# A rewritten instruction order for the first 19 steps of a fused attention and feed-forward kernel

## Chip, core and metric

The kernel runs on one NeuronCore of a Trainium2 chip, as one launch. The metric is the device time of that core in microseconds (us), taken as the median of several runs. Beside the timed runs there is one execution under the hardware profiler, which gives the trace.

## What is computed

Linear attention on eight batches of eight heads, followed by a feed-forward layer over all 4608 rows, in fp32:

```python
q_s = softmax(q, axis=-1)            # exp(q - max) / (sum + 1e-9), over the head dimension
k_s = softmax(k, axis=2)             # over the sequence, 576 rows
kv  = einsum('bhsd,bhse->bhde', k_s, v)
x   = einsum('bhsd,bhde->bhse', q_s, kv)      # -> rows (4608, 512)
h   = x @ w_in                       # (4608, 2048)
g   = h - tanh(h)
out = g @ w_out                      # (4608, 512)
```

The shapes are q, k, v (8, 8, 576, 64), w_in (512, 2048) and w_out (2048, 512). Both weights arrive as 64-bit floats and are split on the chip into a high and a low part.

## The kernel before

**Tiling.** The rows are cut into nine chunks j of 512. For each chunk there are 16 steps f, each of 128 columns of w_in and the matching 128 rows of w_out. Every product of the feed-forward layer is made of three matmuls (high by high, high by low, low by high), so one step is 12 matmuls `ph` (h_mm, x times a piece of w_in) and, two steps later, four groups of three matmuls `po` (o_mm, g times a piece of w_out), one group for each tile of 128 rows. The steps run in this order: chunk 0 with f from 0 to 7, chunk 1 with f from 0 to 15, chunk 0 with f from 8 to 15 (its first half is set aside in DRAM, `ev` and `sv`, and fetched back), then chunks 2 to 8. In the names below ph9 is the ph group of step 9, which is chunk 1 with f=1.

**Names of the parts.** One word of the order is one part of the work, and each part runs on one engine:

- PE (TensorE): `warm13` (13 dummy matmuls), `pm`, `pb`, `pk` (maximum, its broadcast, and k times v of one batch), `pt` (transposes of q), `px` (q times kv), `ph`, `po`.
- SP (SyncE) issues all DMAs: `k0.1`, `q3`, `v1.0` and `ld.i4` (a piece of w_in; `ld.o4` of w_out), `sv`.
- DVE (VectorE): `km`, `mx`, `mh`, `ml` (maximum of k), `ks` (k minus it), `mq`, `sq`, `sa`, `sr` (softmax of q), `sl`, `rs`, `rc`, `kn` (normalising kv), `xl`, the split of a weight (`cl`, `st`), and of each step `g`, `tt`, `gg`, `cp`.
- ACT (ScalarE): `qe`, `ke` (exponentials), `qs`, `xh`, `ev` (copies out of PSUM), the split of a weight (`pr`, `lo`, `ca`), and of each step `u`, `t`, `vv`, `m`, `gh`.
- DVE or POOL (GpSimd): `qu`, `qn`, `sub` (low part of a weight), `gl` (low part of g). A star behind the word puts it on DVE, no star on POOL.

**What sets the order.** ORDER, a list of 576 words, is issued word by word under `tc.manual_schedule` for all five engines; each engine gets its words in this order and executes them in this order, waiting in front of each for its inputs and its buffer. It covers steps 0 to 16 (`PLANNED = 17`) and the split of all 32 weight pieces. From step 17 on only PE and SP keep the written order; the instructions of DVE, ACT and POOL are placed by a planner, which is free to put them between those of ORDER. The attention of chunk 2 (batch 2, and the tile `q_rest`) is written at steps 19.5 to 32 by prepare(2, ...), and the planner places its DVE, ACT and POOL work wherever its inputs are early.

**Buffers that matter.** PSUM has eight banks: two for `ph` (ps_h), four for `po` (ps_o, which before the first `po` hold `pt` and `px`), two for the attention (ps_m). A ph group can begin when the one before the last has been read by u, t, m, g and tt. The step's tiles u, t, g, gh, gl have two buffers each, vv and mk one, the split weights' c three. v_load contains the memset of the ones beside the values (on POOL) and then issues the DMA of the values (on SP).

Of the kernel before, what the change touches and what calls it, by code (L numbers as in the profile page):

```python
# [44 lines left out]
tt4 lo.o7 lo.o6 ld.o8 cp3 qe3 km1.c gh3 cl.o4 ld.o12 km1.d m4 t5 sq3 gl3 ph6 pr.o4 ld.o11 u5 tt5
lo.i9 cl.i7 lo.i8 gg4 ld.o13 pr.i7 st.o4 po3 vv5 cp4 ca.o4 st.i7 ld.i12 gh4 qu2* u6 m5 pm1 gl4*
qe2 ld.i11 mx1 ca.i7 sub.o4* t6 sq2 sub.i7 po4 ld.o9 lo.o11 lo.i12 g5 lo.o8 mh1 cl.o5 lo.o13
ld.o10 ml1 gg5 pr.o5 sa2 pb1 sa3 cp5 vv6 sr2 ld.i10 lo.i11 sr3 ph7 qn5 ks1.0 gh5 m6 gl5 ks1.1
ke1.0 ld.i13 ks1.2 lo.o9 qn6 pk1.0 ke1.1 tt6 qn7 g6 pt6 ke1.2 pk1.1 qs6 st.o5 ld.o15 t7 qn4*
ca.o5 pt5 cl.o6 pk1.2 u7 sub.o5* qs5 ld.i15 sl1 gg6 po5 pr.o6 rs1 lo.i13 cp6 vv7 rc1 st.o6 gh6  # L50
kn1 ca.o6 cl.o7 pt4 m7 g7 sub.o6 pt7 qs4 tt7 qs7 gl6* pr.o7 px6 lo.o15 gg7 lo.i15 st.o7 po6
ld.i14 xh6.0 cp7 xh6.1 xl6.0 gh7 xl6.1 ca.o7 gl7* lo.o10 px4 sub.o7* lo.i10 lo.o12 cl.i8 cl.i9
po7.0 xh4.1 ld.o14 cl.o8 xh4.0 cl.o9 po7.1 xl4.1 pr.i8 xl4.0 pr.i9 po7.2 st.i8 pr.o8 ph8 st.i9
ev.1 ca.i8 cl.o11 sv.1 cl.i11 ca.i9 sub.i8 pr.i11 lo.o14 po7.3 sub.i9* t8 ph9 cl.i13 u8 tt8 m8
g8 vv8 cl.i10 ev.3 gg8 pr.i10 sv.3 cl.o14 ev.2 cp8 ph10 t9 sv.2 st.i10 gh8 tt9 m9 gl8* u9 pr.o14
st.o8 po8.0 t10 g9 vv9 po8.1 tt10 u10 gg9 ph11 ca.o8 g10 vv10 cp9 pr.o9 gg10 gh9 sub.o8* m10
po8.2 gl9* t11 ph12 u11 cp10 ev.0 g11 m11 sv.0 tt11 vv11 cl.o12 ca.i10 gg11 pr.o11 po8.3
sub.i10* u12 ph13 cp11 gh10 st.o11 vv12 gl10* m12 st.i11 t12 pr.o12 g12 po9 t13 tt12 u13 gg12
ca.i11 tt13 vv13 sub.i11 lo.i14 ph14 gh11 cp12 ca.o11 gl11 m13 pr.i13 sub.o11 g13 po10 u14 t14
gg13 tt14 vv14 cp13 ph15 st.o12 gh12 cl.i14 m14 gl12* ca.o12 cl.o15 pr.i14 g14 pr.o15 st.i14  # L60
po11 u15 gg14 t15 sub.o12* ca.i14 cp14 vv15 tt15 m15 ph16 sub.i14* gh13 cl.i12 gl13* pr.i12
st.o14 g15 ca.o14 po12 st.i12 t16 u16 gg15 ca.i12 sub.o14 tt16 vv16 cp15 gh14 sub.i12 m16 gl14*
# [7 lines left out]
def attn_moe_kernel(  # L70
# [533 lines left out]
    def h_step(j: int, f: int):  # L604
        parts = h_parts(j, f)
        last = None
        eng = nc.vector if (j, f) == (NCH - 1, NF - 1) else nc.gpsimd
        for name, part in parts.items():
            if name == "last":
                last = part()  # L610
            elif name == "gl":
                part(eng)
            else:
                part()
        return last
# [120 lines left out]
    done = set()  # L736
    with tc.manual_schedule(engines={ENG.PE, ENG.DVE, ENG.Activation, ENG.Pool, ENG.SP}):
        for name in ORDER.split():
# [12 lines left out]
            done.add(name)  # L751

    pieces = [p for p in pieces if "sub.{}{}".format(*p) not in done]
    loaded = 0

    def pieces_upto(need: int, last):

        nonlocal loaded
        while len(pieces) > need:
            for kind, f in pieces[:2]:  # L760
                if f"ld.{kind}{f}" not in done:
                    ops[f"ld.{kind}{f}"]()
                    done.add(f"ld.{kind}{f}")
            kind, f = pieces.pop(0)
            for part in ("cl", "pr", "lo", "st", "ca", "sub"):
                with tc.issue_after(last.ins):
                    ops[f"{part}.{kind}{f}"](*((nc.gpsimd,) if part == "sub" else ()))
# [60 lines left out]
```

## Time and profile before

| | |
|---|---|
| median of 3 runs | 918.03 us (915.72 to 918.67) |
| profiled execution, device time | 920.28 us |
| its span, first to last instruction | 918.5 us |
| mean granted TensorE clock | 0.99 |
| PE busy | 890.2 us, 97% of the span |
| DVE busy | 615.4 us, 67% |
| ACT busy | 556.1 us, 61% |
| POOL busy | 288.2 us, 31% |

The shares are means over the whole run. The engines' load differs from stretch to stretch, so a view by stretches has to be read beside them. The 1.8 us between the span and the device time lie outside the program's instructions.

### The profile page before, as it was taken

Reading aid. Unit: us, or ns where it says so; the run is one execution under the profiler, and the core shown is the slowest. Engines: PE = TensorE matmul, PEld = TensorE weight load, DVE = VectorE, ACT = ScalarE, POOL = GpSimd, SP = SyncE. Lnnn points to the kernel's source line nnn. Section 1 sums busy time; section 2 is a strip of 40 time slices with the busy share of each in tenths; the row PEclk is TensorE's granted clock in tenths of the full one; section 3 lists DMA queues with packets and bytes.
Section 4 is the critical chain, followed back from the end, with each engine's and each line's share of the span. In section 5 each row is a group of like instructions: output and inputs, shape, how many; then the busy total and the mean of one; then the engine's idle time right before and its main releaser. Section 6 shows DMA issues by size and latency. Waiting matters only on the chain.

```text
span 918.5 us, 13209 instructions
## 1 busy us (share of the span) xinstructions
PE 890.2 (97%) x5034; PEld 721.9 (79%) x5034; DVE 615.4 (67%) x906; ACT 556.1 (61%) x967; POOL 288.2 (31%) x246
## 2 busy tenths in 40 slices
...
GB/s 254 317 305 118 95 82 1 9 61 92 1 126 47 103 1 58 115 12 24 46 61 67 24 46 24 115 0 16 79 24 1 1 70 12 0 1 46 1 1 46
DMA packets 79776, 57.47 MB, mean 63 GB/s; under 512 B 14689, under 2 KB 72033, under 8 KB 79713
## 3 DMA queue, kind: packets, MB, share of 16 engines
...
q14 instruction: 25, 0.20, 0.1%
...
## 4 chain that ended last, share of the span: by engine, by line
PE 77%; DVE 7%; ACT 5%; DMA 4%; issue 4%; POOL 2%; SPq 0%; DVEq 0%; ACTq 0%; POOLq 0%
PE po L635 37%; PE ph L544 35%; PE pk L299 2%; DMA k<-in_k_dram 2%; PE px L465 1%; PE pt L437 1%; DVE g L573 1%; DVE g L565 1%; DVE g L578 1%; DMA spare_q<-in_q_dram 1%; ACT gh L581 1%; DVE t L570 1%; DMA raw_o<-in_moe_w_out_dram 1%; POOL d L267 1%; DMA q<-in_q_dram 1%
## 5 line engine op out<-in xcount | busy, mean ns | idle before, releaser
L635 PE MATMUL po<-w_o,gh 128*128 128x512 f32 x1152 | 361.5, 395 | 1.5 <-DVE w_o L167 1.5
L544 PE MATMUL ph<-xh,w_i 128*128 128x512 f32 x1152 | 317.7, 398 | 10.3 <-ACT mk L559 6.0
L584 POOL TENSOR_TENSOR gl<-g,gh 128x512 fp32r<-128x512 f32 x130 | 172.6, 1328 | 389.7 <-ACT gh L581 373.5
L544 PEld LDWEIGHTS ph<-xh,w_i 128*128 128x128 f32 x1152 | 214.6, 190 | 59.3 <-ACT mk L559 7.3
L635 PEld LDWEIGHTS po<-w_o,gh 128*128 128x128 f32 x1152 | 214.7, 188 | 51.0 <-DVE w_o L167 1.8
L565 DVE SCALAR_TENSOR_TENSOR g<-u,ph 128x512 f32<-128x512 f32 x144 | 98.3, 682 | 219.2 <-ACT t L559 202.2
L635 PE MATMUL po<-w_o,gl 128*128 128x512 f32 x576 | 226.4, 393 | 1.5 <-DVE gl L584 1.5
L581 ACT CAST gh<-g 128x512 fp32r<-128x512 f32 x144 | 89.2, 620 | 177.7 <-DVE g L578 172.6
L544 PE MATMUL ph<-xl,w_i 128*128 128x512 f32 x576 | 157.9, 397 | 0.0
L559 ACT ACTIVATE u<-ph 128x512 f32<-128x512 f32 x144 | 85.8, 596 | 81.4 <-PE ph L544 81.1
L573 DVE SCALAR_TENSOR_TENSOR g<-vv,g 128x512 f32<-128x512 f32 x144 | 120.4, 836 | 20.0 <-ACT vv L559 10.4
L544 PEld LDWEIGHTS ph<-xl,w_i 128*128 128x128 f32 x576 | 109.8, 191 | 25.0 <-DVE xl L486 0.6
L635 PEld LDWEIGHTS po<-w_o,gl 128*128 128x128 f32 x576 | 108.1, 188 | 27.0 <-DVE gl L584 2.4
L578 DVE COPY_PREDICATED g<-mk,t 128x512 f32<-128x512 int32 x144 | 118.8, 825 | 3.3
L559 ACT ACTIVATE vv<-u,b_pa 128x512 f32<-128x512 f32 x144 | 104.5, 726 | 6.9 <-DVE g L573 6.8
L559 ACT ACTIVATE mk<-ph 128x512 int32<-128x512 f32 x144 | 86.2, 599 | 35.9 <-DVE g L565 32.3
L570 DVE TENSOR_TENSOR t<-ph,t 128x512 f32<-128x512 f32 x144 | 98.0, 681 | 4.0 <-ACT mk L559 3.1
L559 ACT ACTIVATE t<-ph 128x512 f32<-128x512 f32 x144 | 85.2, 592 | 1.1 <-PE ph L544 1.1
L389 POOL TENSOR_TENSOR q<-q,mq 128x1024 f32<-128x1024 f32 x14 | 27.7, 1979 | 47.5 <-DVE mq L384 44.6
L423 POOL TENSOR_TENSOR qn<-q,sq 128x512 f32<-128x512 f32 x28 | 31.9, 1142 | 28.1 <-DVE sq L403 14.6
L384 DVE TENSOR_REDUCE mq<-q 128x16 f32<-128x1024 f32 x15 | 18.2, 1216 | 23.9 <-DMA q<-in_q_dram 23.9
L167 POOL TENSOR_TENSOR w_i<-c_i,w_i 128x512 fp32r<-128x512 f32 x10 | 14.5, 1451 | 52.2 <-ACT w_i L163 42.6
...
## 6 DMA issues: line engine op xcount, KB each, us to landing
...
```

What stands on the lines that cost most here:

```text
L299: nc.tensor.matmul(st["pk"][hh * D : (hh + 1) * D, a, j : j + D + 1], kt[:, h, j] if u < NKP else kt[:, h], vt[:, h, j * (D + 1) : (j + 1) ...
L389: eng.tensor_tensor(qf, qf, mq, op=ALU.subtract)
L423: eng.tensor_tensor(qn.rearrange("p a g d -> p g a d"), qt[:, :, j].rearrange("p (g a) d -> p g a d", g=2), sq[:, :, j : j + 1] .broadcast ...
L544: nc.tensor.matmul(ph, w[:, i, c], x[:, c, :], start=(n == 0), stop=(n == len(ops) - 1))
L559: st["last"] = nc.scalar.activation(new(tag, **of), st[src], fn, **kw)
L565: nc.vector.scalar_tensor_tensor(new("g"), st["u"], C2, st["ph"], op0=ALU.mult, op1=ALU.mult)
L570: nc.vector.tensor_tensor(st["t"], st["ph"], st["t"], op=ALU.subtract)
L573: nc.vector.scalar_tensor_tensor(st["g"], st["vv"], PB, st["g"], op0=ALU.add, op1=ALU.mult)
L578: nc.vector.copy_predicated(st["g"], st["mk"], st["t"])
L581: nc.scalar.copy(new("gh", F32R), st["g"])
L584: eng.tensor_tensor(new("gl", F32R), st["g"], st["gh"].bitcast(F32), op=ALU.subtract)
L635: nc.tensor.matmul(po[t], g[:, cols], wt["o", f][:, w], start=(begin and n == 0), stop=(end and n == 2),)
```

## The change

ORDER is written anew. It now has 603 words and covers steps 0 to 18 (`PLANNED = 19`). The memsets of the ones become parts of their own (`vo`), which the order can place ahead of the loads `v`; the memset and the load stay the same instructions. From step 19 to step 31 every instruction of DVE, ACT and POOL is traced under `tc.issue_after` of the last ORDER instruction of its engine, so that the planner can't put it between those of ORDER; this holds for the attention of chunk 2. Two ph groups, of steps 2 and 3, take their PSUM bank from ps_o and not from ps_h. The dummy matmuls fall from 47 to 34 and take another pool once x exists. The function pieces_upto, which had nothing left to do since ORDER splits all 32 pieces, goes.

The core of the diff; of ORDER, the stretch from the start to the first po groups:

```diff
-k0.0 warm13 k0.1 q1 km0.a k0.2 km0.b q0 km0.c mq1 v0.1 km0.d qu1 pm0 v0.2 mq0 warm16 v0.0 mx0
-qu0 qe1 ld.i0 sq1 qe0 ld.o0 mh0 sa1 ml0 sr1 pb0 sq0 qn2 ld.i2 warm1 lo.i0 qn3 ks0.0 pt2 warm1
-qs2 sa0 pt3 ks0.1 ke0.0 ld.i1 warm2 qs3 ks0.2 pk0.0 ke0.1 sr0 ld.i3 cl.i0 qn0* pr.i0 pk0.1 cl.i2
-ke0.2 st.i0 pr.i2 ld.o2 pt0 cl.i1 ca.i0 qn1 pk0.2 lo.i2 warm1 sl0 sub.i0 pr.i1 ld.i4 rs0 pt1 rc0
-qs0 warm2 kn0 qs1 cl.i3 px2 lo.i1 cl.o0 ld.o1 st.i2 pr.o0 px0 st.i1 xh2.1 cl.o2 xh2.0 xl2.1
-ld.i5 ca.i1 warm11 xl2.0 xh0.1 xh0.0 sub.i1* ca.i2 xl0.1 ld.o3 lo.o0 sub.i2 xl0.0 pr.i3 ph0
-lo.i3 k1.0 cl.o1 lo.o1 st.o0 lo.i4 st.i3 ca.o0 cl.i4 ld.o4 cl.o3 ca.i3 sub.o0* pr.i4 ph1 sub.i3*
-u0 st.i4 k1.2 t0 ld.i6 vv0 g0 m0 tt0 ca.i4 gg0 ph2 v1.0 u1 sub.i4 t1 g1 vv1 tt1 lo.o2 ld.i7 gg1
-pr.o2 cp0 u2 st.o2 pr.o1 k1.1 cl.i6 gh0 st.o1 m1 gl0* t2 ph3 q3 cp1 ca.o2 ca.o1 cl.i5 sub.o2*
-gh1 sub.o1 g2 pr.i5 ld.o5 tt2 m2 po0 t3 gl1* vv2 v1.2 km1.a pr.i6 v1.1 gg2 pr.o3 km1.b u3 ph4
...
+vo0.1 q0 mq0 q1 k0.0 mq1 qu0 k0.1 km0.a qe0 sq0 qu1 k0.2 km0.b sa0 km0.c sr0 qe1 ld.i0 ld.i4
+vo0.0 km0.d warm13 pm0 qn0 lo.i4 sq1 lo.i0 mx0 sa1 ld.i2 mh0 sr1 q3 v0.0 ml0 cl.i0 cl.i4 pr.i0
+vo0.2 v0.1 v0.2 cl.i2 pr.i2 warm5 pb0 st.i0 pr.i4 ks0.0 ld.i1 ks0.2 lo.i2 qn1 ke0.0 ks0.1 mq3
+pt0 qn2 st.i2 qu3* warm4 pt1 ke0.2 ke0.1 st.i4 pk0.0 pk0.1 pk0.2 q2 k1.2 qs0 ca.i0 sl0 rs0 cl.i1
+qs1 pt2 ca.i2 qn3 vo1.0 rc0 qe3 lo.i1 kn0 ld.i3 vo1.2 pt3 ld.i5 sub.i2 sub.i0 sq3 qs3 k1.0 pr.i1
+qs2 k1.1 mq2 warm2 px0 px2 warm10 xh0.0 xh0.1 st.i1 qu2 xh2.1 ld.o0 xl0.0 xl0.1 xh2.0 xl2.1
+ca.i1 xl2.0 ld.o1 lo.i3 cl.i5 qe2 lo.i5 cl.i3 ca.i4 pr.i5 ph0 sa3 pr.i3 sub.i1 u0 ld.i6 sr3 m0
+sq2 sa2 km1.a sr2 st.i3 km1.b g0 ld.i7 ph1 km1.c vv0 ca.i3 t0 cl.o0 gg0 u1 pr.o0 km1.d ld.o2 t1
+lo.o0 tt0 cl.o1 vv1 lo.o1 cp0 st.o0 ph2 pm1 sub.i4 mx1 t2 g1 tt1 mh1 qn6 gg1 lo.i6 u2 ca.o0 ml1
+st.i5 gh0 m1 vo1.1 v1.0 cp1 vv2 qn4 pt6 ld.i10 sub.i3 qs6 ca.i5 ph3 qn5 t3 gl0 gh1 sub.i5 pb1
+ks1.2 ks1.0 m2 v1.1 ld.o3 tt2 gl1 ph4 ks1.1 lo.o2 pt4 g2 ke1.0 u3 ke1.2 cl.i7 gg2 qs4 cl.o2 tt3
+ke1.1 u4 vv3 cp2 cl.i6 g3 pr.o1 ld.o5 ph5 st.o1 m3 pr.o2 lo.o3 ca.o1 v1.2 gg3 pr.i6 cl.o3 st.o2
+pk1.0 ld.o4 lo.i7 cl.i10 sub.o1* ld.o10 t5 ld.i12 ca.o2 pt5 sub.o0 ld.o6 qs5 pk1.1 cp3 cl.o5 po0
...
     def warm(n: int):
-        t = ps_h.tile([P, P], F32, name="warm", tag="h")
+        pool, tag = ((ps_m, "m") if po else (ps_o, "o")) if xs else (ps_h, "h")
+        t = pool.tile([P, P], F32, name="warm", tag=tag)
...
-    def v_load(b: int, st: dict, u: int):
+    def v_ones(b: int, st: dict, u: int):
...
     def h_mm(j: int, f: int):
         xh, xl = xs[j]
-        ph = ps_h.tile([P, CH], F32, name=f"ph{j}_{f}", tag="h")
+        pool, tag = (ps_o, "o") if j == 0 and f in (2, 3) else (ps_h, "h")
+        ph = pool.tile([P, CH], F32, name=f"ph{j}_{f}", tag=tag)
...
-    PLANNED, SPREAD = 17, 3
+    PLANNED = 19
...
+            ins = nc.cur_bb.bb.instructions[-1]
+            if ins.engine in (ENG.DVE, ENG.Activation, ENG.Pool):
+                ends[ins.engine] = ins
...
-            last = h_step(j, f)
-            pieces_upto(max(0, left - (left * (n + 1 - PLANNED) + SPREAD - 1) // SPREAD), last)
+            with ExitStack() as behind:
+                for ins in ends.values() if n < 2 * NF else ():
+                    behind.enter_context(tc.issue_after(ins))
+                h_step(j, f)
```

The rest of the new order, by what the prediction uses: PE goes on with `pk1.2 po1 pt7 po2 ph6 px4 ph7 po3 px6 po4 ph8 po5 ph9 po6 po7.0 po7.1 ph10 po7.2 ph11 po7.3 po8.0 po8.1 po8.2 ph12 po8.3 ph13` and ends with `ph18 po15 po16`. POOL has 32 words other than memsets, against 30. DVE has 223, against 215, and ends with `gl18* sub.o15*`; ACT has 221, against 211, and ends with `gh18`.

## Rows read from the trace of the kernel before

**Rows 1.** The page: busy time, share of the span and instructions of each engine.
```profile
PE 890.2 (97%) x5034; PEld 721.9 (79%) x5034; DVE 615.4 (67%) x906; ACT 556.1 (61%) x967; POOL 288.2 (31%) x246
```

**Rows 2.** By stretch: length, busy of each engine (instructions), clock, DMA share, GB/s.
```profile
0.00:30.50 30.50, 23.24 (x266) 22.02 (x266) 20.38 (x36) 15.14 (x24) 10.82 (x19) 0.89 0.98 284
30.50:49.80 19.30, 15.08 (x50) 11.15 (x49) 17.60 (x28) 15.81 (x29) 4.20 (x6) 0.82 0.88 234
49.80:98.50 48.70, 45.27 (x326) 36.08 (x325) 45.92 (x79) 46.94 (x84) 14.85 (x13) 1.00 0.65 217
98.50:118.50 20.00, 17.09 (x64) 12.64 (x63) 16.88 (x28) 16.28 (x30) 0.80 (x1) 0.91 0.23 79
118.50:159.40 40.90, 39.39 (x170) 31.33 (x169) 37.51 (x58) 28.78 (x53) 12.61 (x9) 1.00 0.20 38
159.40:290.00 130.60, 126.25 (x720) 101.43 (x720) 91.23 (x126) 73.91 (x129) 49.26 (x40) 1.00 0.21 59
290.00:910.00 620.00, 620.00 (x3431) 504.45 (x3430) 383.80 (x552) 357.68 (x621) 195.67 (x160) 1.00 0.13 35
```

**Rows 3.** Chain that ended last, near 218 us: start, us, what.
```profile
217.69 2.72 PE ph L544 x12
```

**Rows 4.** Waits, 30 to 160 us: us in total, times, longest.
```profile
PE ph L544 <- ACT mk L559: 6.0, 3, 2.2
...
PE ph L544 <- DVE t L570: 2.0, 1, 2.0
...
DVE km L226 <- DMA k<-in_k_dram: 1.0, 1, 1.0
```

**Rows 5.** Timeline around the k load of batch 2: start, us, engine, line.
```profile
106.18 0.38 SPq L189 DMA_DIRECT2D k<-in_k_dram  x1
...
110.30 0.69 DVE L223 TENSOR_TENSOR km<-k 128x512 f32<-128x512 f32 x1 [1.08 <-DMA k<-in_k_dram]
...
112.26 0.62 ACT L581 CAST gh<-g 128x512 fp32r<-128x512 f32 x1 [1.33 <-DVE g L578]
...
113.43 1.36 PE L544 MATMUL ph<-xh,w_i 128*128 128x512 f32 x4 [2.09 <-ACT mk L559]
```

**Rows 6.** Two short stretches, columns as in Rows 2: ph12, then part of po15.
```profile
113.43:117.87 4.44, 4.44 (x12) 3.51 (x13) 3.78 (x7) 3.70 (x7) 0.00 (x0) 0.62 0.16 61
149.65:154.01 4.36, 3.05 (x13) 2.17 (x12) 4.26 (x7) 2.75 (x5) 1.29 (x2) 1.00 0.01 4
```

**Rows 7.** Timeline of the start, 0 to 31 us.
```profile
13.92 1.22 DVE L397 TENSOR_REDUCE sq<-spare_q 128x16 f32<-128x1024 f32 x1 [0.27 <-ACT spare_q L392]
...
23.86 0.68 PE L299 MATMUL pk<-vr,kr 64*64 64x65 f32 x16
...
27.95 2.72 PE L183 MATMUL warm<-ident 128*128 128x128 f32 x22
...
28.11 0.42 DVE L145 TENSOR_SCALAR raw_o<-raw_o 128x512 f32<-128x512 f32 x1
...
30.52 1.21 PE L544 MATMUL ph<-xh,w_i 128*128 128x512 f32 x4
```

**Rows 8.** Timeline of DVE and POOL at three places, 22 to 153 us.
```profile
22.90 1.21 DVE L156 SCALAR_TENSOR_TENSOR c_i<-raw_i 128x512 uint32<-128x512 uint32 x1 [0.19 <-ACT raw_i L149]
...
38.33 1.28 POOL L167 TENSOR_TENSOR w_i<-c_i,w_i 128x512 fp32r<-128x512 f32 x1 [5.90 <-ACT w_i L163]
38.38 1.77 DVE L573 SCALAR_TENSOR_TENSOR g<-vv,g 128x512 f32<-128x512 f32 x1
...
40.08 0.68 DVE L565 SCALAR_TENSOR_TENSOR g<-u,ph 128x512 f32<-128x512 f32 x1
...
41.28 0.68 DVE L573 SCALAR_TENSOR_TENSOR g<-vv,g 128x512 f32<-128x512 f32 x1
...
152.23 2.42 DVE L156 SCALAR_TENSOR_TENSOR c_o<-raw_o 128x512 uint32<-128x512 uint32 x2
```

**Rows 9.** Timeline of PE at the maximum of batch 2.
```profile
173.14 0.60 PE L235 MATMUL pm<-ident,km 128*128 128x128 f32 x4
```

More of the change, by code (lines that the diff above doesn't have):

```diff
@@ L45 @@
[L45 to L62, printed above, removed]
@@ new lines @@
+pr.o4 kn1 ld.o7 st.o3 px4 cl.o6 vv5 gh4 cl.i12 st.o4 ca.o3 gg5 ca.o4 xh4.1 sub.o3* st.o5 gl4* u6
+sub.i7 cp5 xl4.1 xh4.0 cl.o9 t6 ph7 u7 vv6 lo.o7 po3 xl4.0 tt6 t7 px6 ca.o5 gh5 g6 m6 xh6.0
+ld.i9 xh6.1 ld.i13 pr.o6 pr.i12 gg6 sub.o4 xl6.0 xl6.1 lo.i10 lo.o6 ld.o8 po4 cl.o12 cl.o7
+sub.o5* cp6 cl.i9 ld.i11 pr.o7 gl5 g7 ph8 st.o6 vv7 lo.i11 m7 ld.i15 tt7 gg7 po5 gh6 pr.i10 cp7
+gl6* st.i10 u8 ca.o6 st.o7 ph9 ld.i14 ld.i8 sub.o6* lo.i12 vv8 gh7 g8 po6 pr.i9 t8 lo.i15 t9 u9
+tt8 ca.o7 pr.o12 gg8 gl7* m8 sub.o7* vv9 lo.i9 po7.0 cl.i15 cl.i8 pr.i15 tt9 st.i12 cp8 ld.o15
@@ new lines @@
+cl.i13 lo.o10 ld.o11 po7.1 ld.o14 gh8 lo.i8 m9 st.i15 ph10 gl8* g9 cl.o15 ev.0 po7.2 cl.i14 sv.0
+gg9 ca.i12 u10 cl.o8 cp9 ph11 cl.i11 ev.2 ev.1 t10 ca.i15 vv10 g10 po7.3 tt10 po8.0 m10 sub.i15
+cl.o11 cl.o14 po8.1 pr.o10 gg10 t11 gh9 ev.3 u11 ca.i10 gl9* pr.o8 pr.i8 cp10 g11 po8.2 tt11
+vv11 m11 sub.i12 ph12 lo.o12 st.o10 gg11 st.i9 sub.i10 ca.o10 t12 lo.o8 lo.o14 st.i8 po8.3 gh10
+ph13 cp11 ca.i9 u12 m12 ld.o13 po9 ca.i8 lo.i14 t13 sub.i9* sub.o10* gl10* pr.i11 sv.3 tt12 vv12
+g12 st.o12 gh11 gg12 ca.o12 u13 st.i11 pr.o11 gl11* po10 cp12 pr.o9 m13 sub.o12 tt13 vv13 ca.i11
@@ new lines @@
+ph14 pr.i14 lo.i13 g13 gg13 po11 sub.i8* u14 sub.i11* cp13 gh12 gl12* t14 st.o8 ph15 lo.o9
+pr.o15 g14 sv.1 po12 m14 gh13 tt14 lo.o11 st.o9 vv14 ca.o8 ph16 gl13* gg14 pr.i13 u15 sv.2 vv15
+pr.o14 st.o11 g15 cp14 gh14 t15 sub.o8 lo.o15 u16 po13 m15 gg15 tt15 vv16 t16 cp15 ca.o11 gl14
+cl.o13 sub.o11 tt16 g16 ca.o9 st.i14 ph17 gg16 lo.o13 st.i13 gh15 po14 gl15* m16 ca.i14 cp16
+ca.i13 u17 g17 ph18 t17 sub.i13* st.o14 vv17 gg17 gh16 ca.o14 tt17 sub.o14* sub.o9* u18 po15
+gl16* t18 st.o15 tt18 po16 m17 pr.o13 ca.o15 vv18 st.o13 cp17 gh17 g18 sub.i14 gg18 m18 ca.o13
@@ L66 @@
+cp18 gl17* sub.o13* gh18 gl18* sub.o15*
 """
@@ L177, in attn_moe_kernel @@
     REST = S - 2 * P * NKP
+    gs = {}
+    po = {}
+    xs = {}
     def warm(n: int):
-        t = ps_h.tile([P, P], F32, name="warm", tag="h")
+        pool, tag = ((ps_m, "m") if po else (ps_o, "o")) if xs else (ps_h, "h")
+        t = pool.tile([P, P], F32, name="warm", tag=tag)
         for _ in range(n):
@@ L498, in prepare @@
                 put(0, lambda u=u: k_load(b, st, u))
-            put(0, lambda: v_load(b, st, 0))
-            put(0, lambda: v_load(b, st, NKP))
+            for u in (0, NKP):
+                for part in (v_ones, v_load):
+                    put(0, lambda u=u, part=part: part(b, st, u))
             for n in range(4):
@@ L509, in prepare @@
             put(KX + 7, lambda: kv_mm(b, st, 0))
-            put(KX + 7, lambda: v_load(b, st, 1))
+            for part in (v_ones, v_load):
+                put(KX + 7, lambda part=part: part(b, st, 1))
             put(KX + 10, lambda: kv_mm(b, st, 1))
@@ L558, in act @@
             of = {"dt": kw.pop("dt", F32)} | ({"bufs": kw.pop("bufs")} if "bufs" in kw else {})
-            st["last"] = nc.scalar.activation(new(tag, **of), st[src], fn, **kw)
+            nc.scalar.activation(new(tag, **of), st[src], fn, **kw)
         def ph():
@@ L605, in h_step @@
         parts = h_parts(j, f)
-        last = None
         eng = nc.vector if (j, f) == (NCH - 1, NF - 1) else nc.gpsimd
         for name, part in parts.items():
[L609 to L615, printed above, removed]
+            part(*((eng,) if name == "gl" else ()))
     dram = ctx.enter_context(tc.tile_pool(name="dram", bufs=1, space=bass.MemoryType.DRAM))
@@ L735, in attn_moe_kernel @@
     ENG = mybir.EngineType
-    done = set()
+    ends = {}
     with tc.manual_schedule(engines={ENG.PE, ENG.DVE, ENG.Activation, ENG.Pool, ENG.SP}):
@@ L750, in attn_moe_kernel @@
             ops[name](*eng)
[L751 to L767, printed above, removed]
+            ins = nc.cur_bb.bb.instructions[-1]
+            if ins.engine in (ENG.DVE, ENG.Activation, ENG.Pool):
+                ends[ins.engine] = ins
     calls = {}
```

38 lines of the change are left out of this document (17 added, 21 removed).

## The prediction

> **What bounds the kernel now.** I read the page first, then the busy time by stretch, the chain that ended last, the waits, and the timeline of the first 160 us. On the page PE is busy for 97% of the span, so only PE's idle and slow time can be won, and the question is where it lies [rows 1]. The stretches answer it: from 290 to 910 us PE has no idle time at all, in 620.0 us [rows 2]. Nothing there can be gained, and the change doesn't touch it. The losses lie ahead. At full clock a group of twelve matmuls takes 2.72 us [rows 3]. By that measure:
>
> - 30.5 to 49.8 us holds four ph groups, 10.9 us of work in 19.3, so 8.4 are lost. PE waits there for m and tt of the steps before, because only two PSUM banks serve ph, and the clock falls to a mean of 0.82 [rows 2, 4].
> - 49.8 to 98.5 us: 48.7 less 45.3 busy at clock 1.00, so 3.4 lost [rows 2].
> - 98.5 to 118.5 us: 64 matmuls, 14.5 us of work in 20.0, so 5.5 lost [rows 2].
> - 118.5 to 159.4 us: 40.9 less 39.4, so 1.5 lost [rows 2].
>
> That is 18.8 us between the first ph and the 17th po, beside 30.5 us ahead of the first ph. From 159.4 to 290 us another 4.3 are idle [rows 2]. In the stretch from 49.8 to 98.5 us ACT is busy for 46.9 of 48.7 us and DVE for 45.9 [rows 2]: whatever is put in front there pushes something else back. The order can win time by doing early only what PE needs next.
>
> **The start: no change, with a possible loss.** The new order loads q first, and puts i0, i4, i2 and q3 ahead of the values v. Up to the last v stand ten transfers of 512 KB and two of 128 KB, 5.5 MB; at 284 GB/s [rows 2] that is 19.4 us, plus some 3 us until the first data comes, so v is there at about 22.5 us. In the kernel before pk of the rest began at 23.86 us [rows 7]; in the new one it can begin at about the same time, since k itself still comes within the first five transfers. The chain behind it (kn, px, xh) is as long as before. Eleven dummy matmuls, 2.72 us, ended just ahead of ph0 at 30.52 [rows 7]; ten end there now. I take ph0 at 30.5, 0 us. The bounds: 1 us earlier, the dummy matmul and the shorter queue; 3 us later, if PE, which has 5 dummies and not 16 ahead of pb0, runs pk and px (some 5 us) at the half clock.
>
> **The first ph groups: 2.6 us won of 8.4.** With four PSUM banks instead of two, ph0 to ph3 no longer wait for tt and m. But the new order puts pm1 ahead of ph3 and pb1 ahead of ph4, and PE works in order: all ph behind them wait with them. PE reaches pm1 three groups after ph0, at 38.7 us. Pm1 needs km1.d, the 15th DVE instruction behind the last xl (about 31.0 us): seven of full width at 0.60 us from one start to the next [rows 8], one reduction of 1.22, three clamps of 0.42 [rows 7] and four small ones of about 0.1, 7.1 us in all, so 38.1 us. Pb1 needs ml1, ten instructions on: seven of full width, one clamp, two small, 4.8 us, so about 42.9. PE has ph3 (2.72) and eight 128-wide matmuls of pm1 and pt6 ahead of it, which at 2.72/22 each [rows 7] are 1.0, so it is there at 42.4 and waits 0.5 us. That is without blocks. The blocks are the unknown: between ph0 and po0 the old order has two POOL instructions, the new one ten (sub.i1, sub.i4, qn6, qn4, sub.i3, qn5, gl0, sub.i5, gl1, sub.o0). A DVE instruction with both operands in SBUF that begins beside one takes 1.77 us and not 0.68 [rows 8]. Between 22 and 153 us fifteen DVE rows are longer than their like, by 11.9 us in all; the first and the last of them stand in [rows 8]. That is 0.4 us for each of the 30 POOL instructions of the old order. Up to seven of the ten can fall ahead of ml1. Their blocks cost nothing at the least, 7 × 1.1 = 7.7 us at the most, and 2.8 by the mean, which I take, since most DVE instructions there read PSUM as g does, unslowed at 0.68 [rows 8]. I add the 0.5 from above, 0.8 for po0, whose last two tiles need the banks that ph2 and ph3 now hold (0 to 2), and one spell at half clock: ph12, after a wait of 2.09, took 4.44 us instead of 2.72 [rows 5, 6], so 1.7 (0 to 3.4). Loss 5.8, bounds 0.5 to 13.6.
>
> The Trainium skill (SBUF — State Buffer, Who interferes with whom) says that a VectorE instruction with two SBUF inputs and a GpSimd instruction that reads SBUF exclude each other for the whole instruction, whichever comes first. The trace agrees where the two rows at 38 us overlap. If every one of the ten met such an instruction, the sum would be that of the POOL rival below.
>
> **49.8 to 98.5 us: 1.4 won of 3.4.** The new order has done six ph and most of chunk 1's attention by po0, so the later attention no longer competes with them. What stays is px4 behind kn1, the 102nd word of DVE, with little slack. I take 2.0 lost (0 to 5, again by blocks).
>
> **98.5 to 118.5 us: 4.3 won of 5.5.** The planner put km2.a between two instructions of ORDER, and it waited 1.08 us for a load issued only at 106.18; cp9 behind it, then gh9 (idle 1.33), then m10 came late, and ph12 waited 2.09 for m [rows 5]. Then the clock fell, mean 0.62 over ph12, which took 1.7 us too long [rows 6]. Together 3.8 us hang on this. The second wait of km was 1.0 [rows 4]. Queued behind ORDER, km2 can't do this any more. I take 1.2 lost (0 to 3).
>
> **118.5 to 159.4 us: 0.8 won of 1.5.** The idle time is nearly all in po15, 4.36 us less 3.05 busy, 1.3 [rows 6], waiting for gl15 at the crowded end of ORDER. Two more planned steps move this end back. I take 0.7 (0 to 2).
>
> **What moves back.** The third chunk's attention now starts after the last DVE word, sub.o15*. Before, DVE's last words of ORDER ended near 154.7 us [rows 8]. Eight more words add 4.8, the attention that moves out takes some 4.5 away, and with PE 9 us ahead part of DVE's waits go: I take 150, at the latest 155. PE reaches pm2, at 173.1 us before [rows 9], at about 164. In these 14 us some 4.5 us of DVE work (km2, the softmax of q_rest) must fit beside steps 19 to 21, where the mean load is 91.2 in 130.6 us, 70% [rows 2], its own attention included. It fits, barely: 0 us, bounds −1 (part of the 4.3 idle goes) and +3. The memsets are not a cost: six of 0.1 us on POOL, which idles 69% of the time [rows 1]; if POOL were full they would cost 0.6.
>
> **Sum.** Losses 5.8 + 2.0 + 1.2 + 0.7 = 9.7 against 18.8: 9.1 us less. The profiled execution took 920.28 us (span 918.5 and 1.8 outside), so 911.2; it lies 2.25 above the median of the runs. Against the median of 918.03 the forecast is 908.9 us, say 909.
>
> **The rivals.**
> - *PE nearly without gaps.* If DVE's blocks fall on instructions with slack and the clock stays up, only about 3 of the 18.8 us stay: 902 us. For it: ACT and DVE together carry less in front of po8 than before (132 ACT words ahead of gh8, against 144). Against it: both are at 95% from 49.8 to 98.5 us [rows 2].
> - *The front only trades one wait for another.* Pm1, pb1 and pk1 wait for DVE as ph2 and ph3 did, and the start loses 1 to 2 us to the clock. Then only the two later terms stay, 4.3 + 0.8 = 5.1 less 2: 915 us. For it: the wide bounds of the first term.
> - *POOL blocks DVE (the other side).* Place: steps 0 to 18. After the start 26 POOL instructions read SBUF. At 0.4 us each they cost DVE 10 us, about what they cost before, and it keeps pace. At 1.1 each they cost 29: DVE ends near 169 us, 18 later, po16 ends no earlier than before, and pm2 at 173 finds km2 unfinished by 3 to 5 us, which PE waits out: 921 us, slower. It decides from about 0.75 us for each, where DVE, 9 us later, eats the gain. For it: ten POOL instructions between ph0 and po0 and not two. Against it: the fifteen rows of before, and that PSUM readers aren't slowed [rows 8].
> - *Without effect* (the edges or banks change nothing that PE waits for) I hold unlikely, since the waits for m, tt and km are in the rows [rows 4, 5]; it would be 918 and is counted with the POOL rival.
>
> **Chances and range.** The forecast (909, by itself 905 to 913) 0.52; PE without gaps 0.15; the trade at the front 0.16; POOL or no effect 0.17. A difference under 0.3%, 2.75 us, can't be told from none. The forecast and the first rival are faster, the trade half faster and half the same, the last one 0.08 the same and 0.09 slower: faster 0.74, same 0.17, slower 0.09. The range 901 to 918 leaves out about 0.07 below and 0.11 above.
>
> **What would show it.** Right: ph0 near 30.5; ph0 to ph2 back to back; waits of PE at pm1 and pb1 on DVE km and ml of 1 to 4 us; no DVE wait for the k load of batch 2 ahead of step 18; po16 done near 150 us; an unchanged stretch behind 290. Wrong: ph0 behind 32 us with pk and px at half clock; many DVE rows of 1.7 us beside POOL; or PE waiting at pm2, pk2 or px8 for km2 and what follows.

## The result, and the profile after

The changed kernel takes 906.87 us (median of 4 runs, 906.29 to 909.11) against 918.35 for the kernel before on the same chip (median of 4): a ratio of 0.9884, 95% interval 0.9857 to 0.9911. That is 11.5 us faster where 9 were forecast, and inside the range. The profiled execution was the longest of the four, 909.11 us, with a span of 907.3. One execution of run 11 below took 2252.07 us and is left out of that run's times.

The busy time by stretch of the kernel after, over the same stretches and with the same columns as [rows 2]:

```profile
0.00:30.50 30.50, 19.96 (x235) 18.89 (x236) 24.30 (x36) 17.16 (x27) 13.98 (x24) 0.89 0.99 254
30.50:49.80 19.30, 16.65 (x83) 13.24 (x82) 18.90 (x33) 16.50 (x31) 14.08 (x10) 1.00 1.12 339
49.80:98.50 48.70, 47.11 (x325) 36.46 (x324) 46.54 (x81) 45.37 (x84) 9.39 (x8) 1.00 0.51 182
98.50:118.50 20.00, 19.66 (x84) 15.61 (x85) 18.55 (x30) 19.06 (x37) 5.45 (x4) 1.00 0.46 139
118.50:159.40 40.90, 38.82 (x171) 31.74 (x171) 36.35 (x57) 31.07 (x56) 7.98 (x7) 1.00 0.11 23
159.40:290.00 130.60, 126.93 (x763) 102.20 (x762) 89.44 (x132) 72.23 (x125) 47.69 (x41) 0.99 0.21 59
```

In this execution PE works at full clock from ph0 up to 159.4 us, and its idle time is length less busy: 2.65, 1.59, 0.34 and 2.08 us, 6.7 in all, where the same stretches of before lost 18.8 [rows 2, 3]. What is left is named by the waits of PE, 28 to 160 us (us in total, times, longest):

```profile
PE pm L246 <- DVE km L240: 2.1, 1, 2.1
PE ph L555 <- DVE t L581: 2.1, 1, 2.1
...
PE pb L268 <- DVE mh L255: 0.3, 1, 0.3
PE pb L268 <- DVE ml L259: 0.3, 1, 0.3
```

The waits for m, tt and km's load in [rows 4] are gone from their places; the first of the new ones is the wait at pm1 that the prediction described. The timeline of that place:

```profile
31.04 1.17 PE L555 MATMUL ph<-xh,w_i 128*128 128x512 f32 x4
...
34.86 1.57 POOL L434 TENSOR_TENSOR qn<-q,sq 128x512 f32<-128x512 f32 x1
...
35.60 1.37 DVE L157 SCALAR_TENSOR_TENSOR c_i<-raw_i 128x512 uint32<-128x512 uint32 x1
...
36.44 1.45 POOL L434 TENSOR_TENSOR qn<-q,sq 128x512 f32<-128x512 f32 x1
36.90 1.53 DVE L237 TENSOR_TENSOR km<-km,k 128x512 f32<-128x512 f32 x1
...
37.85 1.75 POOL L168 TENSOR_TENSOR w_i<-c_i,w_i 128x512 fp32r<-128x512 f32 x1
...
38.36 0.68 DVE L576 SCALAR_TENSOR_TENSOR g<-u,ph 128x512 f32<-128x512 f32 x1
...
38.95 1.19 DVE L237 TENSOR_TENSOR km<-km,k 128x512 f32<-128x512 f32 x1
...
41.01 0.67 DVE L240 TENSOR_TENSOR km<-km,kr 64x512 f32<-64x512 f32 x1
...
41.74 0.44 PE L246 MATMUL pm<-ident,km 128*128 128x128 f32 x2 [2.09 <-DVE km L240]
```

Ph0 to ph2 run back to back from 31.04 us. Beside POOL's instructions three of DVE's, c_i and two parts of km, take 1.37, 1.53 and 1.19 us and not 0.67, 2.1 us more in all. The last part of km begins at 41.01 us, and PE, ready 2.09 us before km is done, waits. Two waits further on were not priced in the prediction. The first is new, in the timeline at ph17:

```profile
128.44 1.40 POOL L168 TENSOR_TENSOR w_o<-c_o,w_o 128x512 fp32r<-128x512 f32 x1 [10.58 <-ACT w_o L164]
128.60 1.78 DVE L157 SCALAR_TENSOR_TENSOR c_o<-raw_o 128x512 uint32<-128x512 uint32 x1
...
134.40 0.69 DVE L581 TENSOR_TENSOR t<-ph,t 128x512 f32<-128x512 f32 x1 [2.19 <-ACT mk L570]
...
135.15 1.20 PE L555 MATMUL ph<-xh,w_i 128*128 128x512 f32 x4 [2.08 <-DVE t L581]
```

A DVE instruction that begins 0.16 us behind one of POOL takes 1.78 us; g, gh, t and m of step 15 come behind it; tt15 waits 2.19 us for m15, and ph17 2.08 for tt15. The second is at the first group of chunk 2, ph32:

```profile
230.21 0.62 ACT L592 CAST gh<-g 128x512 fp32r<-128x512 f32 x1 [1.64 <-DVE g L589]
230.73 1.07 ACT L493 CAST xh<-px 128x512 fp32r<-128x512 f32 x2
...
231.36 1.30 PE L555 MATMUL ph<-xh,w_i 128*128 128x512 f32 x4 [2.11 <-ACT xh L493]
```

The planner put gh31 in front of xh on ACT, so xh came late although px had ended at 229.25 (it began at 228.15 and took 1.10 us). This wait isn't new. The kernel before has the same order and a shorter wait, in its timeline:

```profile
241.92 0.62 ACT L581 CAST gh<-g 128x512 fp32r<-128x512 f32 x1 [1.65 <-DVE g L578]
242.45 1.07 ACT L484 CAST xh<-px 128x512 fp32r<-128x512 f32 x2
...
243.08 1.23 PE L544 MATMUL ph<-xh,w_i 128*128 128x512 f32 x4 [1.52 <-ACT xh L484]
```

In the kernel after ph32 waited 2.11 us, 0.6 more, and over it the clock fell to a mean of 0.62, as over ph12 before [rows 6]:

```profile
231.36:235.83 4.47, 4.47 (x12) 3.42 (x13) 1.27 (x2) 0.44 (x1) 0.82 (x1) 0.62 0.01 4
```

**Where the time came from.** PE's finished matmuls (all but the dummies, each kind at its mean distance from one start to the next, and interpolated) were counted in both traces, and the times at which the same work was done were compared. This table gives by how many us the kernel after, and a second profile of it (the last run below), lead the kernel before at a point of before's time:

```
point of before, us   31     49.8   98.5   118.5  159.4  290    end
forecast              0      2.6    4.0    8.3    9.1    9.1    9.1
after                -0.5    5.2    6.8   11.1   10.6   10.2   11.2
after, again         -0.9    3.4    6.4   10.7   10.1   12.4   13.3
```

The spans give the last column: 918.5 less 907.3 is 11.2, and less 905.2 is 13.3. The profiled execution of before, 920.28 us, lies some 2 us above the medians of that kernel (917.93 to 918.49 us in the sets of runs here), that of after 2.2 us above its own, and the second one of after 0.6 us below its own. So 11.2 is comparable with the 11.5 of the medians, while 13.3, like other leads over this one profile, can be some 2 us too high.

### The profile page after: what moved, and what is told of

Its sections match the earlier page's. It is cut to its first block, busy times and chain, and to the rows that moved or that the text cites. A ratio compares the mean times of both kernels' runs of the same rounds, so it can differ in the third digit from the quotient of the medians.

```text
span 907.3 us, 13173 instructions
## 1 busy us (share of the span) xinstructions
PE 881.8 (97%) x5008; PEld 716.9 (79%) x5008; DVE 616.7 (68%) x906; ACT 554.4 (61%) x967; POOL 288.8 (32%) x246
## 4 chain that ended last, share of the span: by engine, by line
PE 72%; DVE 12%; ACT 6%; DMA 4%; issue 3%; POOL 1%; SPq 1%; DVEq 0%; ACTq 0%; POOLq 0%
PE po L638 34%; PE ph L555 34%; DMA q<-in_q_dram 2%; DVE g L589 2%; DVE t L581 2%; PE pk L310 2%; DVE g L576 2%; DVE g L584 2%; PE px L474 1%; PE pt L448 1%; DMA k<-in_k_dram 1%; ACT gh L592 1%; DMA raw_i<-in_moe_w_in_dram 1%; ACT mk L570 1%; ACT t L570 1%
## 5 line engine op out<-in xcount | busy, mean ns | idle before, releaser
L584 DVE SCALAR_TENSOR_TENSOR g<-vv,g 128x512 f32<-128x512 f32 x144 | 117.4, 815 | 18.8 <-ACT vv L570 8.3
L434 POOL TENSOR_TENSOR qn<-q,sq 128x512 f32<-128x512 f32 x30 | 34.6, 1153 | 27.2 <-PE pt L448 12.9
L168 POOL TENSOR_TENSOR w_i<-c_i,w_i 128x512 fp32r<-128x512 f32 x12 | 18.3, 1531 | 39.1 <-ACT w_i L164 28.9
```

Source lines behind the costliest of these rows:

```text
L168: eng.tensor_tensor(w[:, 1], st["c"].bitcast(F32), w[:, 0].bitcast(F32), op=ALU.subtract)
L434: eng.tensor_tensor(qn.rearrange("p a g d -> p g a d"), qt[:, :, j].rearrange("p (g a) d -> p g a d", g=2), sq[:, :, j : j + 1] .broadcast ...
L584: nc.vector.scalar_tensor_tensor(st["g"], st["vv"], PB, st["g"], op0=ALU.add, op1=ALU.mult)
```

## The experiments

Each run is compared with the kernel before on the same chip; "the new order" is the kernel after.

**1. The new order without the edges.**

```diff
-                for ins in ends.values() if n < 2 * NF else ():
+                for ins in ():
```

> The changed kernel without the edges that keep the third chunk's attention behind the planned instructions; the planner then puts the four km and the softmax of q_rest of batch 2 between the split of w_i and w_o around steps 12 to 13 on DVE. If those insertions cost what the trace of before showed (3.8 us at ph12), this run is 2 to 5 us slower than the changed kernel (906.9), so 909 to 912, with DVE waiting for the k or q_rest load and PE waiting behind it between 105 and 125 us. If the edges only move DVE work that has to be done anyway, it takes 906 to 908.

913.80 us (median of 5 rounds, 911.74 to 914.21); ratio to before 0.9947 (0.9934 to 0.9960). So the edges are worth 6 to 7 us by the medians (913.80 less 907.52 and less 906.87) and 5 to 6 by the ratios, more than the 2 to 5 expected. The planner did in the new order what it had done in the old one [rows 5], one step later. DVE and PE in that run's timeline:

```profile
112.84 0.69 DVE L234 TENSOR_TENSOR km<-k 128x512 f32<-128x512 f32 x1 [2.28 <-DMA k<-in_k_dram]
...
115.20 0.69 DVE L237 TENSOR_TENSOR km<-km,k 128x512 f32<-128x512 f32 x1 [1.67 <-DMA k<-in_k_dram]
...
117.02 0.69 DVE L595 TENSOR_TENSOR gl<-g,gh 128x512 fp32r<-128x512 f32 x1
...
117.76 0.80 PE L638 MATMUL po<-w_o,gl 128*128 128x512 f32 x1 [3.13 <-DVE gl L595]
```

Km of batch 2 waits 2.28 and then 1.67 us for its loads with gl10 behind it on DVE, and po10 waits 3.13 us for gl10. The lead over before falls from 10.8 us at 118.5 to 3.1 at 159.4, some of it by waits like this of q_rest's instructions (ACT 3.5 us, DVE 2.8).

**2. The new order with ph2 and ph3 back on the two banks of ph.**

```diff
-        pool, tag = (ps_o, "o") if j == 0 and f in (2, 3) else (ps_h, "h")
+        pool, tag = ps_h, "h"
```

> The changed kernel with ph2 and ph3 back on the two ps_h banks. If the two extra banks are what lets ph0 to ph3 run on, ph2 waits for tt0 (41.6 us in the changed kernel's trace, 4.9 us after PE is free) and ph3 for tt1 and m1 (46 us), PE falls 3 to 7 us behind at po0, with a spell at half clock, and the whole takes 910 to 914. If pm1 and pb1, which wait for the same DVE queue, set the pace anyway, PE only waits at another place and it takes 906.5 to 908.5.

925.39 us (923.48 to 925.74); ratio to before 1.0071 (1.0059 to 1.0083). This is slower than the kernel before, and 17 to 18 us slower than the kernel after, where 3 to 7 were expected. Its timeline shows why:

```profile
42.74 2.08 PE L555 MATMUL ph<-xh,w_i 128*128 128x512 f32 x4 [5.41 <-DVE t L581]
...
47.20 0.60 PE L246 MATMUL pm<-ident,km 128*128 128x128 f32 x4
...
47.83 0.69 DVE L250 TENSOR_REDUCE mx<-pm 128x4 f32<-128x512 f32 x1 [3.56 <-PE pm L246]
```

Ph2 waits 5.41 us for tt0, which in the new order stands behind km1 on DVE, and pm1 stands behind ph2 on PE. So chunk 1's attention starts 5.5 us later (pm1 at 47.20, not 41.74), DVE itself waits 3.56 us for it, and the waits go round: PE waits 5.4, 2.4, 4.2 and 3.8 us ahead of ph2, ph3, ph4 and ph5, with three stretches of 6.83 us at half clock among them.

**3. Only ph2 on a bank of po, in the new order.**

```diff
-        pool, tag = (ps_o, "o") if j == 0 and f in (2, 3) else (ps_h, "h")
+        pool, tag = (ps_o, "o") if (j, f) == (0, 2) else (ps_h, "h")
```

> The kernel after, with ph2 on a bank of po and ph3 back among the two of ph. Theory: the 18.5 us that both banks are worth hang on ph2, which stands ahead of pm1 and so of chunk 1's whole attention; ph3 stands behind pm1, at 42.6 us, when tt0 has nearly set its bank free, so the time is 908 to 911, and PE's waits lie at ph3 or ph4 with under 3 us in all. Rival, that each bank is worth its half, since ph4 then waits for tt1 as ph3 for tt0 and pb1 and pk1 come as late as with two banks: 914 to 918, with waits at pb1, ph4 and ph5 of 2 to 5 us each.

914.57 us (912.95 to 915.36); ratio to before 0.9964 (0.9950 to 0.9977). The time is the rival's, the place neither's. Ph3 starts at 42.88 without a wait of its own, as the theory said; the bank that it takes is missing two groups on:

```profile
57.08 0.60 ACT L570 ACTIVATE mk<-ph 128x512 int32<-128x512 f32 x1 [1.15 <-DVE g L576]
...
57.73 0.79 PE L555 MATMUL ph<-xh,w_i 128*128 128x512 f32 x1 [6.73 <-ACT mk L570]
```

Ph5 now needs the bank of ph3 and not of ph1, and m3 comes only at 57.08: 6.73 us of waiting, and half clock from 53.96 to 60.79. Ph3's bank is worth 7 us (914.57 less 907.52, the kernel after on the same chip) and ph2's another 10 to 11 (925.39 less 914.57, from two chips, is 10.8; the ratios give 9.8).

**4. The old order with ph2 on a bank of po.** (With ph3 there too, gh2 would wait for po0 and po0's banks for m3, which stands behind gh2.)

```diff
-        ph = ps_h.tile([P, CH], F32, name=f"ph{j}_{f}", tag="h")
+        pool, tag = (ps_o, "o") if (j, f) == (0, 2) else (ps_h, "h")
+        ph = pool.tile([P, CH], F32, name=f"ph{j}_{f}", tag=tag)
```

> The kernel before with one edit: ph2 alone takes its bank from the four of po (with ph3 too the old order would lock up). If two banks are the limit of the first steps, ph2 starts at 36.5 and not 38.5 us, ph3 follows, the half clock spells at 39 and 46 us go, and 3 to 6 us are won (ratio 0.993 to 0.997). If DVE and ACT set the pace of the first steps, PE waits at ph3, ph4 or po0 instead and the ratio is 0.998 to 1.001.

918.62 us; ratio 0.9998 (0.9985 to 1.0010). PE leads before by 8.1 us at 49.8 us, and by 0.4 at 98.5. In this run's waits of PE, 28 to 98 us, ph and po wait for what ACT and DVE have ready no sooner:

```profile
PE ph L545 <- ACT mk L560: 2.3, 1, 2.3
PE po L636 <- DVE w_o L167: 1.7, 1, 1.7
PE po L636 <- ACT gh L582: 1.6, 1, 1.6
```

So a bank that is worth 10 to 11 us in the new order is worth nothing in the old.

**5. The old order with the edges on everything planned.** The same edges as in the change, on all that is planned for steps 17 to 31.

```diff
+            with ExitStack() as behind:
+                for ins in ends.values() if n < 2 * NF else ():
+                    behind.enter_context(tc.issue_after(ins))
                 last = h_step(j, f)
...
                         call()
```

> The kernel before, old order and all, with the edges alone: batch 2's km and the softmax of q_rest can't stand among the planned instructions. If the DVE wait for the k load (1.1 us, then ph12 2.1 us late and at half clock) cost 3.8 us, it gains 3 to 5 us on the kernel before (ratio 0.995 to 0.997), and ph12 takes 2.75 us. If the time comes back at the end of the plan or at pm2, the ratio is 0.999 to 1.002.

920.77 us (919.98 to 922.14); ratio 1.0031 (1.0018 to 1.0044), slower. From 98.5 to 118.5 us the stall is gone (PE busy for 18.55 us at clock 1.00, before 17.09 at 0.91 [rows 2]), and the lead over the profile of before is 4.9 us at 159.4. Then it falls to −0.9 in one place, in the timeline of that run:

```profile
153.46 3.29 POOL L167 TENSOR_TENSOR w_i<-c_i,w_i 128x512 fp32r<-128x512 f32 x2 [1.28 <-ACT w_i L163]
...
153.96 3.33 DVE L226 TENSOR_TENSOR km<-km,k 128x512 f32<-128x512 f32 x2
157.22 0.67 DVE L565 SCALAR_TENSOR_TENSOR g<-u,ph 128x512 f32<-128x512 f32 x1
...
160.34 1.22 PE L544 MATMUL ph<-xh,w_i 128*128 128x512 f32 x2 [5.65 <-DVE t L570]
```

In the old order the plan begins at step 17, so g and tt of steps 17 and 18 stand behind the same edges as km of batch 2. DVE does km first, and ph19 waits 5.65 us for tt17. Two parts of km stand beside POOL's split of a weight and take 3.33 us, where each alone takes some 0.67; so some 2 us of the delay lie there. At its end this execution leads the profile of before by 0.3 us, although its median is 2.8 us longer: that profile is some 2 us above its median, and this one 0.8 below its own.

**6. The old order with the edges on the attention alone.**

```diff
+                with ExitStack() as behind:
+                    for ins in ends.values() if n < 2 * NF else ():
+                        behind.enter_context(tc.issue_after(ins))
                     for call in calls.pop(2 * n + half, ()):
                         call()
```

> The kernel before, with the edges put around the third chunk's attention calls alone (not around the MoE instructions of the planned steps, which in the old order begin at step 17). Theory, that the wait of ph12 comes from km2 among the written instructions: the 3.8 us of that place go and nothing comes in their place, so about 914 us against 918, with 98.5 to 118.5 us at full clock and no wait of DVE for the k load ahead of step 18. Rival, that the edges are only worth something together with the new order's place of the plan's start (step 19): km2 and the exponentials now run in one lump behind the last word and hold back g and tt of steps 17 and 18, so PE waits 4 to 6 us near 155 to 160 us instead and the time is 917 to 921.

914.78 us (913.56 to 916.11) against 918.49; ratio 0.9960 (0.9945 to 0.9976). That is 3.7 us, where the prediction priced the one stall at 3.8 from [rows 5, 6], and up to 159.4 us nothing takes its place:

```profile
98.50:118.50 20.00, 18.55 (x77) 13.94 (x76) 17.59 (x30) 18.23 (x35) 1.22 (x1) 1.00 0.28 92
118.50:159.40 40.90, 40.90 (x179) 33.40 (x178) 38.39 (x55) 30.43 (x55) 17.16 (x13) 1.00 0.04 11
```

The agreement is partly luck: the lead over the profile of before grows by 3.0 us from 98.5 to 118.5, by 2.2 more to 159.4, where the wait at po15 goes too, and 0.7 are lost again by 200. Together with run 5 this explains the two further steps in the written order (17 and 18): with them there is no instruction of those steps that the edges could hold back. The new order with the old length was not run. With 914.78 us for the old order and these edges, the rest of the change (the new order with its banks) is worth 7 to 8 us; the old order with edges and bank together was not run.

**7 to 9. Three waits of the new order taken away, one by one.** Pm1 behind ph3 and pb1 behind ph4 (with sub.i3 and what POOL does ahead of it moved up); tt15 straight behind t15; px of the third chunk's second pair one step earlier.

```diff
-ph2 pm1 sub.i4 mx1 t2 g1 ... ph3 qn5 t3 gl0 gh1 sub.i5 pb1 ks1.2 ... gl1 ph4
+ph2 sub.i4 qn6 vo1.1 qn4 sub.i3 ph3 pm1 mx1 t2 g1 ... sub.i5 ph4 pb1 ks1.2
```
```diff
-t15 sub.o8 lo.o15 u16 po13 m15 gg15 tt15 vv16
+t15 tt15 m15 sub.o8 lo.o15 u16 po13 gg15 vv16
```
```diff
-            return begin - 9 + at if at < 9 else begin + (at - 9) * 12 // 15
+            return begin - 9 + at if at < 9 else min(begin + (at - 9) * 12 // 15, 4 * NF - 3)
```

> The kernel after, with pm1 behind ph3 and pb1 behind ph4 on PE (and sub.i3 ahead of ph3's place, the first instructions of POOL in the order sub.i4, qn6, qn4, sub.i3). Theory, that in the new order the front loses only what pm1 and pb1 wait for km and ml: both waits, 2.1 and 0.6 us, go, and the time is 2 to 2.7 us shorter than the kernel after, about 904.5 against 907. Rival, that from 50 to 98 us ACT and DVE, busy nine tenths of it, set the pace and not PE: the 2.7 us come back as waits for gh or tt ahead of 118 us and the time stays within 1 us of the kernel after.

> The kernel after, with tt15 and m15 straight behind t15 in the written order, ahead of lo.o15, u16 and po13. Theory, that ph17's wait of 2.08 us for t is the order's: tt15 waited 2.19 us for m15, which stands on ACT behind lo.o15 and u16. Tt15 then needs only t15 and the wait of ph17 shrinks by 0.8 to 2 us, so about 905 to 906 against 907. Rival, that the late instruction is gh14, held back by a POOL block of DVE: the wait moves by under 0.3 us, and so does the time.

> The kernel after, with the last product of the third chunk's attention (px of its second pair) one step earlier, ahead of the 32nd ph and its po. Theory, that ph32's wait of 2.11 us for xh and the spell at half clock behind it (1.7 us) are the planner's order of px and xh: both go, and the time is 3 to 3.8 us shorter than the kernel after, about 903.5 against 907. Rival, that q's normalisation and transposition are late: px itself waits then, and the time stays within 1 us of the kernel after or is longer.

Measured 907.27, 907.61 and 905.94 us (ratios 0.9882, 0.9882, 0.9864, each within 0.0017), against 906.87 and 907.52 for the kernel after. Pm1's edit is the rival's case, in its stretches:

```profile
30.50:49.80 19.30, 18.79 (x95) 15.21 (x94) 18.57 (x32) 16.54 (x31) 13.64 (x10) 1.00 1.10 338
49.80:98.50 48.70, 45.68 (x313) 34.48 (x311) 46.48 (x81) 45.31 (x84) 9.53 (x8) 1.00 0.53 184
```

The two waits are gone from the first stretch (0.5 us idle, not 2.65), and PE's lead over before at 49.8 us is 7.5 us and not 5.2; at 80 us it is 6.4, against 6.5 for the kernel after. From 49.8 on DVE and ACT are busy 46.5 and 45.3 of 48.7 us, and PE takes their pace. Tt15's edit comes to the same. The one wait of 2.1 us becomes two, of 1.2 at most:

```profile
PE ph L554 <- ACT mk L569: 2.1, 2, 1.2
```

Now m15 is late behind tt15, and the next step too. Neither reason fits whole: tt15's place was the cause of the one wait, but step 15 as a whole comes late, and another order inside it only shares that out. Px's edit has its effect where it was expected, from 159.4 to 290 us:

```profile
159.40:290.00 130.60, 129.47 (x783) 105.14 (x782) 91.08 (x132) 74.76 (x129) 49.63 (x42) 1.00 0.22 64
```

PE idles 1.1 us there instead of 3.7, and xh's wait is gone. The gain is 0.9 to 1.6 us by the medians and 2.0 by the spans (903.2 against 905.2 in run 12), not 3 to 3.8: the spell at half clock that was counted with it isn't there in each execution of the kernel after (run 12).

**10. The ones set straight ahead of their loads.** In the new order, each `vo` next to its `v`:

```diff
-vo0.0 km0.d warm13 pm0 ... q3 v0.0 ml0 cl.i0
+km0.d warm13 pm0 ... q3 vo0.0 v0.0 ml0 cl.i0
```

> The kernel after, with each setting of the ones moved back in the written order to straight ahead of its load of v (still before the qn or sub words that stand behind it). Theory: SP issues v's first load 4 us later, behind qn0 on POOL, but four transfers of 512 KB are still under way then, so v lands when it did, 19.5 us, ph0 begins within 0.4 us of 31.0 and the time stays within 1.5 us of the kernel after. Rival, that the split is what gives the early start room: SP stands behind POOL's qn instructions, the weights and v land 2 to 4 us later, and the time is 2 us or more longer.

908.38 us (906.53 to 909.06) against 907.52: no difference beyond the runs' spread, as the theory has it. SP issues the first load of v at 14.76 instead of 10.12 us, and v lands at 19.41 instead of 19.52. At 14.76 two transfers issued ahead of it have yet to land (at 15.81 and 17.61), not four as the theory had it, and two are enough. That part of the change is worth nothing in this order. The timeline of SP in this run:

```profile
14.76 0.37 SPq L221 DMA_DIRECT2D v<-in_v_dram  x1
```

**11. All three edits of runs 7 to 9 together** (their diffs are those above).

> The three edits of the runs before together on the kernel after: pm1 behind ph3 and pb1 behind ph4, tt15 straight behind t15, the last px of the third chunk one step earlier. Theory: the first two only move a wait to the next place where ACT and DVE are late (between 50 and 98 us, and behind po13) and are worth nothing together either; px10's edit stands on PE's own order and keeps its 1 to 2 us, so 905 to 906, as with px10's edit alone. Rival: the first two came to nothing only because each met the other's wait; together they give 2 to 3 us more, 902 to 903.

905.94 us (median of five, 905.10 to 906.59); ratio 0.9871 (0.9851 to 0.9891). It is the theory's case: the same time as px's edit alone. These two are the lowest of all twelve, but the intervals of their ratios overlap that of the kernel after.

**12. The kernel after again.**

> The kernel after once more, unchanged, on the same chip as the three beside it: 906 to 908, by which they are read. Its profile tells whether the spell at half clock behind ph32's wait comes each time or only sometimes.

907.52 us (906.90 to 908.31); ratio 0.9889 (0.9871 to 0.9907). Its profile has no spell at half clock behind ph32, but one over ph3, where the first profile had none:

```profile
43.26:46.67 3.41, 3.41 (x9) 2.64 (x8) 3.41 (x8) 3.41 (x7) 2.05 (x2) 0.50 1.16 327
```

## Why the prediction was right, step by step

- **The start** was put at 0, bounds −1 to +3. The last v landed at 22.49 us (22.5 forecast). Ph0 came at 31.04 us against 30.52, and at 31.44 in the second profile: right in kind, 0.5 to 0.9 us too low.
- **The first ph groups** were to win 2.6 us. They won 5.7 in the first profile (from −0.5 to 5.2) and 4.3 in the second. Two waits were sized well: 2.8 us of POOL's blocks ahead of ml1 and 0.5 at pb1 were forecast, 2.09 at pm1 and 0.56 at pb1 measured, and the DVE instructions that are lengthened ahead of ml1 are 2.7 us too long together (the three in the timeline above and a clamp at 31.89 us). Mis-sized were the other two terms: po0 didn't wait for its banks at all (0.8 forecast), and the spell at half clock (1.7) was absent in one profile and cost 0.6 us in the other (ph4 began at 48.25 us and not at 47.29, and 0.4 of that was there at ph0).
- **The reason given for the 2.8 us** doesn't hold. It was that most DVE instructions there read PSUM; of the 25 between the last xl and ml1 only five do (g0, tt0, mx1, g1, tt1). The row that it cites for them, 40.08 us in [rows 8], has no POOL instruction beside it: the one at 38.33 had ended at 39.61. The row at 38.36 us of the kernel after, 0.68 us beside POOL's w_i, is one that shows it. So the size of this term was in part luck.
- **49.8 to 98.5 us**: 1.4 forecast, 1.6 measured in the first profile and 3.0 in the second, which stood 1.8 lower at 49.8. So these two terms can't be told apart as the sum has them: what is won or lost by 49.8 us evens out behind it. Runs 2 and 3 show that the banks are needed for the lead of 6.8 us at 98.5 (without both it is −11.2 there, with ph2's alone 0.2), but runs 4 and 7 show that PE's lead at 49.8 us doesn't carry it: 8.1 us there left 0.4 in the old order, and 7.5 instead of 5.2 left nothing more in the new one. What fits is the work of DVE: up to 98.5 us it is busy for 89.7 us in the kernel after and 83.9 before, and 3.9 of these 5.8 us more lie ahead of 30.5 us [rows 2]. That this sets the lead is argued, not shown.
- **98.5 to 118.5 us**: 4.3 forecast, 4.3 measured (11.1 less 6.8). That km2 behind the DMA was the cause is shown from both sides: run 6 keeps it out of the old order and wins 3.7 us in all, run 1 lets it back into the new one and loses 6 to 7.
- **118.5 to 159.4 us**: 0.8 forecast, −0.5 measured. The old wait at po15 went, and ph17's of 2.08 us came. The prediction looked for trouble from km2 and not among step 15's own instructions. One POOL block of 1.1 us stands ahead of them in the timeline; that it started the wait is read from there and no run took it away. Run 8 shows that the order of t, lo, u and m on ACT alone doesn't cure it.
- **What moves back** was put at 0 (−1 to +3). It was 0.4 lost in the first profile and 2.2 won in the second. Both gain 1.5 to 1.7 us from 159.4 to 240 us, more than the 1 us that was the bound for the idle time of before. At ph32 the first profile loses 2.2 again: 0.6 by the longer wait and 1.6 by the slow clock, which the second doesn't have.
- **Behind 290 us** nothing was to change. The lead grew by another 1.0 us, spread over the whole stretch. In all ten profiles of the new order with or without an edit it is 0.8 to 1.0, in the three of the old order (runs 4 to 6) 0.0. The matmuls there are the same in the same order. Matched one by one from 307 us on, no distance from one start to the next shrinks by more than 0.012 us; those between two po matmuls add up to 0.9 us won, those between two ph matmuls to 0.3 lost. So it isn't a wait of PE. Why they differ is open.

So the span shrank by 11.2 us and not by 9.1: 2.8 more by 98.5, 1.3 less to 159.4, 0.4 less to 290, 1.0 more behind it. The errors partly cancel, and that the total came so near is partly luck. The POOL rival failed: from 18 to 160 us, 16 DVE instructions are longer than the shortest of their like, by 11.1 us for 28 POOL instructions (memsets not counted), 0.40 us each against 0.4 in the forecast and 0.75 where it would have decided. (The forecast divided by all 30 of the old order; 23 of them ran in its stretch from 22 to 153 us, which gives 0.52.) The rule of the Trainium skill that was quoted with it (SBUF — State Buffer, Who interferes with whom) agrees where instructions meet, as in the 1.53 and 1.78 us rows above.

What the prediction missed altogether is that the parts hold each other up. It summed them as if each had its own worth. Measured one by one, by medians: the new order without the edges gives 4.1 us (913.80 against 917.93 on that chip), without the banks it costs 7.5 (925.39 against 917.93), the bank of ph2 in the old order gives nothing beyond the runs' spread (ratio 0.9998), the edges in the old order 3.7 or −2.8 by where they are put. The new order, with km1 ahead of tt0, costs time without the banks and wins with them. Edges on everything planned cost time in the old order, which ends with step 16, and pay in the new one, which ends with step 18; on the attention alone they pay in the old order too.
